# First gate projection by pairs of row chunks (0 and 2, then 1 and 3) through a strided moving operand, with the late transposes copied by two engines

## Chip, cores, metric

One core of one Trainium2 chip. The metric is the device time of one execution in microseconds (us); the span of a trace is about 1.3 us shorter. Before: 164.19 us, median of three runs (164.17 to 164.63). A change counts as faster or slower beyond 2%.

In the traces PE is TensorE, PEld its weight loads, DVE VectorE, ACT ScalarE, and SP the engine that issues most of the DMAs. Tile `pt` is a transposed chunk in PSUM, `xT` its copy in SBUF, `pw` the output of the warm-ups. k counts the five pieces of 128 input columns (KD = 5); the chunks of 128 rows are numbered 0 to 3.

## The reference

```python
def reference(x, w_gate, w_up, w_down):      # x 1x2048x640, w_gate and w_up 640x1536, w_down 1536x640, all bf16
    g = silu(x @ w_gate)
    u = x @ w_up
    return (g * u) @ w_down
```

## The kernel before

The kernel works on four blocks of 512 rows of x; in each, twelve times, a gate projection `pg` (5 matmuls, one for each 128 of the 640 input columns), an up projection `pu`, silu on ScalarE, a product on VectorE; then the down projection. The x of blocks 1 to 3 is transposed by DMA. The 512 rows of block 0 come as four chunks of 128 rows, are transposed on TensorE and copied out of PSUM, because the first matmul waits for them. Warm-up matmuls on a tile of ones fill TensorE until data are there. "Second block" below means the second 128 columns of the weights, that is the second pg and pu.

```python
    N_WARM = 20
    W_CHUNKS = [(0, 1), (1, 3), (3, 6), (6, 9), (9, 12)]
    # ... (tiles and views cut)
    queues = (nc.sync, nc.scalar)
    halves = ((0, KD // 2 + 1), (KD // 2 + 1, KD))
    for c in (0, 1):                                   # SP: chunks 0, 1; ACT: chunks 2, 3
        for i, eng in enumerate(queues):
            load_x(eng, c + 2 * i, c + 2 * i + 1)
    for dst, src in ((wg_sb, wg_v), (wu_sb, wu_v)):    # weights of the first block
        for eng, (k0, k1) in zip(queues, halves):
            eng.dma_start(out=dst[:, k0:k1, wslice(0, 1)], in_=src[:, k0:k1, wslice(0, 1)])
    load_w(nc.sync, wg_sb, wg_v, *W_CHUNKS[1])         # second and third block
    # ... (silu table, further loads, helpers cut)

    def transpose_chunk(c, parts):
        c_sl = slice(c * P, (c + 1) * P)
        for copy, tag, k0, k1 in parts:
            pt = psum.tile([P, k1 - k0, P], bf16, tag=tag, name="pt")
            for kd in range(k0, k1):
                nc.tensor.transpose(out=pt[:, kd - k0, :],
                                    in_=x_sb[:, c, kd * P : (kd + 1) * P], identity=ident[:])
            copy(out=xT[:, k0:k1, c_sl], in_=pt[:])

    # ... in the loop, first projection only:
                h = (SUB - 1) * P
                warm(N_WARM)
                for n, c in enumerate((0, 2, 1)):
                    transpose_chunk(c, [(nc.vector.tensor_copy, ("po_a", "po_b")[n % 2], 0, KD)])
                transpose_chunk(SUB - 1, [(nc.vector.tensor_copy, "po_b", 0, 2),
                                          (nc.scalar.copy, "po_a", 2, KD)])
                warm(2)
                proj(pg, wg_sb, fc, sb, 0, h)          # columns of chunks 0, 1, 2
                proj(pg, wg_sb, fc, sb, h, S_BLK)      # chunk 3
                proj(pu, wu_sb, fc, sb, 0, S_BLK)
```

## Time and profile before

| | before |
|---|---|
| time (median), span of the trace | 164.19 us, 163.1 us (of an execution of 164.41 us) |
| TensorE busy | 159.1 us (98%) |
| first gate matmul starts | 5.39 us |
| second block's first up matmul starts | 8.64 us |
| from there to the end | 154.46 us |

### The profile page before, as it was taken

The page shows a single profiled execution, that of the slowest core. Times are in us where ns is not written, and L with a number is a line of the kernel's source. Part 1 is how long each engine was busy: PE and PEld are TensorE (multiplying, and loading weights), DVE is VectorE, ACT ScalarE, POOL GpSimd, SP SyncE. Part 2 cuts the span into 40 slices and gives each one's busy share as a digit, 9 for nine tenths or more (in the row PEclk, how much of TensorE's full clock was granted, in tenths as well). Part 3 has the DMA queues.
Part 4 walks back from the last instruction along what each step waited for, and adds up shares of the span by engine and source line. Part 5 has one row for each costly group of instructions (what it writes and reads, how often), then busy time and mean ns, then how long its engine had stood idle before and what let it go on. Part 6 is the DMA issues. An engine that isn't in the chain of part 4 may idle for free.

```text
span 163.1 us, 1864 instructions
## 1 busy us (share of the span) xinstructions
PE 159.1 (98%) x764; PEld 75.2 (46%) x779; DVE 37.8 (23%) x58; ACT 42.2 (26%) x71; POOL 0.6 (0%) x6
## 2 busy tenths in 40 slices
PE   8899999999999999999999999999999999999994
PEld 7544444444444444444444444444444444445442
DVE  2323333310013333311003333331001333332000
ACT  3222222212232222221222222221214222222121
POOL 1000000000000000000000000000000000000000
DMA  7999999803200000003110000000320000000312
GB/s 212 274 333 330 361 245 187 152 6 60 67 32 0 0 0 0 4 0 34 64 64 0 2 4 0 0 0 3 62 68 32 0 0 0 0 0 4 54 34 72
DMA packets 26888, 11.26 MB, mean 69 GB/s; under 512 B 17664, under 2 KB 26880, under 8 KB 26880
## 3 DMA queue, kind: packets, MB, share of 16 engines
q1 hardware_dynamic: 17968, 10.16, 22.9%
q10 hardware_dynamic: 8912, 0.98, 3.9%
q8 instruction: 6, 0.10, 0.3%
q14 instruction: 2, 0.02, 0.0%
HBM read 6.55 MB, written 2.62 MB: 56 GB/s over the span
## 4 chain that ended last, share of the span: by engine, by line
PE 95%; DMA 2%; issue 1%; DVE 0%; SPq 0%
PE pg L134 32%; PE pu L134 31%; PE po_a L204 25%; PE po_t L180 6%; DMA x_sb<-in_x_dram 2%; PE po_b L217 0%; PE pt L125 0%; DVE xT L130 0%; SPq L74 0%; DVE ot_b L225 0%
## 5 line engine op out<-in xcount | busy, mean ns | idle before, releaser
L134 PE MATMUL pg<-xT,wg_sb 128*128 128x512 bf16 (+2 forms) x245 | 59.7, 375 | 0.2 <-DVE xT L130 0.2
L134 PE MATMUL pu<-xT,wu_sb 128*128 128x512 bf16 x230 | 59.0, 379 | 0.5
L172 DVE TENSOR_TENSOR aT<-sg,pu 128x512 bf16<-128x512 f32 x48 | 33.0, 687 | 100.8 <-PE pu L134 100.8
L171 ACT ACTIVATE sg<-pg 128x512 f32<-128x512 f32 x48 | 28.7, 597 | 71.1 <-PE pg L134 71.1
L204 PE MATMUL po_a<-wd_sb,aT 128*128 128x512 bf16 x188 | 41.9, 379 | 0.2
L134 PEld LDWEIGHTS <-wg_sb 128*128 128x128 bf16 x245 | 23.8, 98 | 28.4 <-DMA wg_sb<-in_w_gate_dram 0.4
L134 PEld LDWEIGHTS <-wu_sb 128*128 128x128 bf16 x240 | 23.4, 98 | 28.1
L204 PEld LDWEIGHTS <-aT 128*128 128x128 bf16 x192 | 18.8, 98 | 22.5
L212 ACT CAST ot<-po_a 128x512 bf16<-128x512 f32 x16 | 9.4, 585 | 32.4 <-PE po_a L204 19.2
L180 PE MATMUL po_t<-aT,wd_sb 128*128 128x512 bf16 (+1 forms) x47 | 10.3, 366 | 0.1
L180 PEld LDWEIGHTS <-wd_sb 128*128 128x128 bf16 x48 | 4.7, 98 | 5.1
L189 ACT CAST ot_t<-po_t 128x512 bf16<-128x512 f32 (+1 forms) x4 | 2.2, 558 | 11.6 <-PE po_t L180 11.6
L190 DVE STREAM_TRANSPOSE ot_q<-ot_t 128x512 bf16<-128x512 bf16 (+1 forms) x4 | 2.7, 678 | 9.1 <-ACT ot_t L189 9.1
L103 PE MATMUL pw<-ones 128*128 128x128 bf16 x22 | 2.6, 302 | 0.4 <-DVE ones L78 0.4
L225 DVE CAST ot_b<-po_b 128x128 bf16<-128x128 f32 x1 | 0.3, 292 | 9.9 <-PE po_b L217 9.9
L125 PE MATMUL pt<-ident,x_sb 128*128 128x128 bf16 x20 | 2.0, 269 | 0.5 <-DMA x_sb<-in_x_dram 0.5
L130 DVE COPY xT<-pt 128x640 bf16<-128x640 bf16 (+1 forms) x4 | 1.7, 439 | 3.5 <-PE pt L125 3.5
L103 PEld LDWEIGHTS <-ones 128*128 128x128 bf16 x22 | 2.2, 139 | 0.4 <-DVE ones L78 0.4
L125 PEld LDWEIGHTS <-x_sb 128*128 128x128 bf16 x20 | 1.6, 122 | 0.9 <-DMA x_sb<-in_x_dram 0.8
L89 ACT ACT_TABLE_LOAD x1 | 1.3, 1283 | 2.0 <-issue 2.0
L130 ACT COPY xT<-pt 128x384 bf16<-128x384 bf16 x1 | 0.5, 479 | 1.6 <-PE pt L125 1.6
L217 PEld LDWEIGHTS <-aT 128*128 128x128 bf16 x12 | 0.8, 98 | 0.2
(9 smaller groups left out, 2.1 us busy)
## 6 DMA issues: line engine op xcount, KB each, us to landing
out_dram<-ot SPq DMA_DIRECT2D x16, 128.0 KB, 1.7
wd_sb<-in_w_down_dram SPq DMA_DIRECT2D x1, 1920.0 KB, 11.8
wg_sb<-in_w_gate_dram SPq DMA_DIRECT2D x3, 480.0 KB, 7.1
wu_sb<-in_w_up_dram SPq DMA_DIRECT2D x3, 480.0 KB, 7.8
out_dram<-ot_q ACTq DMA_DIRECT2D x12, 32.0 KB, 1.9
x_sb<-in_x_dram SPq DMA_DIRECT2D x2, 160.0 KB, 3.1
x_sb<-in_x_dram ACTq DMA_DIRECT2D x2, 160.0 KB, 3.3
wg_sb<-in_w_gate_dram SPq DMA_DIRECT2D x1, 320.0 KB, 4.3
```

The source lines that it names most:

```text
L89: nc.scalar.activation(silu_first[:], ones[:, 0:1], ACT.Silu)
L103: nc.tensor.matmul(pw[:, 0:P], lhsT=ones[:], rhs=ones[:], start=True, stop=True)
L125: nc.tensor.transpose(out=pt[:, kd - k0, :], in_=x_sb[:, c, kd * P : (kd + 1) * P], identity=ident[:],)
L130: copy(out=xT[:, k0:k1, c_sl], in_=pt[:])
L134: nc.tensor.matmul(ps[:, c0:c1], lhsT=w_sb[:, kd, fc * P : (fc + 1) * P], rhs=xT[:, kd, sb * S_BLK + c0 : sb * S_BLK + c1], start=(kd == 0 ...
L171: nc.scalar.activation(sg[:], pg[:], ACT.Silu)
L172: nc.vector.tensor_tensor(out=aT[:, fc, s_sl], in0=sg[:], in1=pu[:], op=ALU.mult)
L180: nc.tensor.matmul(po_t[:], lhsT=wd_sb[:, kf, DA:D], rhs=aT[:, kf, sb * S_BLK : sb * S_BLK + n_t], start=(kf == 0), stop=(kf == KF - 1),)
L189: nc.scalar.copy(ot_t[:], po_t[:])
L190: nc.vector.transpose(out=ot_q[:], in_=ot_t[:])
L204: nc.tensor.matmul(po_a[:], lhsT=aT[:, kf, s0 : s0 + P], rhs=wd_sb[:, kf, 0:DA], start=(kf == 0), stop=(kf == KF - 1),)
L212: nc.scalar.copy(ot[:], po_a[:])
```

## The change

Its intent: start the gate projection on the two chunks that arrive first (0 and 2), while the copies of the two late ones (1 and 3) still run, and let ScalarE and VectorE share these copies. Four warm-ups move into the gap before the late chunks. The assertion on SUB is left out here.

```diff
-    N_WARM = 20
+    N_WARM, N_GAP = 18, 4
...
+    def proj_pair(ps, w_sb, fc, sb, b):
+        def pair(ap):
+            return ap.rearrange("p (a b c) -> p b a c", b=2, c=P)[:, b]
+        for kd in range(KD):
+            nc.tensor.matmul(
+                pair(ps[:]),
+                lhsT=w_sb[:, kd, fc * P : (fc + 1) * P],
+                rhs=pair(xT[:, kd, sb * S_BLK : (sb + 1) * S_BLK]),
+                start=(kd == 0),
+                stop=(kd == KD - 1),
+            )
...
-                h = (SUB - 1) * P
+                dve, act = nc.vector.tensor_copy, nc.scalar.copy
                 warm(N_WARM)
-                for n, c in enumerate((0, 2, 1)):
-                    transpose_chunk(
-                        c, [(nc.vector.tensor_copy, ("po_a", "po_b")[n % 2], 0, KD)]
-                    )
-                transpose_chunk(
-                    SUB - 1,
-                    [
-                        (nc.vector.tensor_copy, "po_b", 0, 2),
-                        (nc.scalar.copy, "po_a", 2, KD),
-                    ],
-                )
+                transpose_chunk(0, [(dve, "po_a", 0, KD)])
+                transpose_chunk(2, [(dve, "po_b", 0, KD)])
+                warm(N_GAP)
+                for c in (1, 3):
+                    transpose_chunk(c, [(act, "po_a", 0, 2), (dve, "po_b", 2, KD)])
                 warm(2)
-                proj(pg, wg_sb, fc, sb, 0, h)
-                proj(pg, wg_sb, fc, sb, h, S_BLK)
+                proj_pair(pg, wg_sb, fc, sb, 0)
+                proj_pair(pg, wg_sb, fc, sb, 1)
                 proj(pu, wu_sb, fc, sb, 0, S_BLK)
```

## The prediction

> **What bounds the kernel now.** I read the page's busy table and chain first, then the waits of the two TensorE rows, then the first 8 us in order of time, because the diff touches only what runs before the second projection.
>
> From the page:
>
> ```profile
> PE 159.1 (98%) x764; PEld 75.2 (46%) x779; DVE 37.8 (23%) x58; ACT 42.2 (26%) x71; POOL 0.6 (0%) x6
> ...
> PE 95%; DMA 2%; issue 1%; DVE 0%; SPq 0%
> ```
>
> TensorE is busy for 98% of the 163.1 us span and carries 95% of the chain that ended last. The waits of PE over the whole run are 0.4 us at the start, 0.5 us for x, and this, its only wait after 5.3 us:
>
> ```profile
> PE pg L134 <- DVE xT L130: 0.2, 1, 0.2
> ```
>
> So past 5.39 us TensorE is a solid row: a change in the start can only move that row rigidly, by the change in the moment when the first up projection (pu) starts. The chain at the start:
>
> ```profile
> 0.46 3.81 DMA x_sb<-in_x_dram
> 4.26 0.05 issue
> 4.31 0.51 PE pt L125 x5
> 4.82 0.02 issue
> 4.84 0.50 DVE xT L130
> 5.35 0.04 issue
> 5.39 1.25 PE pg L134 x10
> ```
>
> Read alone, this says: x chunk 1 lands at 4.27, five transposes, a 0.50 us VectorE copy, then the gate projection. That is what the change attacks. But the row of weight loads over 4.2 to 7.7 us says something the chain hides:
>
> ```profile
> 4.30 0.60 PEld L125 LDWEIGHTS <-x_sb 128*128 128x128 bf16 x10 [0.80 <-DMA x_sb<-in_x_dram]
> 4.87 0.15 PEld L103 LDWEIGHTS <-ones 128*128 128x128 bf16 x2
> 5.37 1.09 PEld L134 LDWEIGHTS <-wg_sb 128*128 128x128 bf16 x10 [0.35 <-DMA wg_sb<-in_w_gate_dram]
> ```
>
> The first gate weights were themselves awaited: the load started at 5.37, released by the DMA of w_gate, 0.02 us before the matmul that the copy released. Two waits end together, and the chain shows only the later. The landings confirm it (issue start plus time to landing, from the views of the issues): w_gate k 0 to 2, issued 0.91, 4.4 us, lands 5.31; k 3 and 4, issued 1.03, 4.5 us, lands 5.53. The w_up pieces: issued 1.39, 4.9 us, lands 6.29; issued 1.52, 4.5 us, lands 6.02. The x chunks: 0 at 2.5, 2 at 2.83, 1 at 4.27, 3 at about 4.5. (Times to landing are rounded to 0.1 us.)
>
> Could the weights come sooner? The 16 DMA engines are full meanwhile (columns: PE, PEld, DVE, ACT, POOL busy, clock, DMA share, GB/s):
>
> ```profile
> 2.50:3.60 1.10, 1.10 (x12) 1.01 (x10) 0.32 (x1) 1.03 (x2) 0.00 (x0) 1.00 1.04 313
> 3.60:4.30 0.70, 0.18 (x2) 0.00 (x0) 0.66 (x2) 0.00 (x0) 0.00 (x0) 1.00 1.03 233
> ```
>
> and the diff touches no transfer.
>
> **What the Trainium skill says.** "TensorE: Matmul & The Clock Gate", section "Back-to-back issue gap": an isolated warm gap of N/2.4 + 2.5 ns. The trace agrees with that form: 5 matmuls of 512 columns take 1.08 us in the chain, 216 ns each; and pg's 5x384 + 5x128 from 5.39 to the last result at 6.64 fit 5x162.5 + 5x55.8 = 1.09 us of gaps plus the drain. I use 109 ns for N=256 (an estimate by that formula). The same page, Part 1: the clock is at half rate until about 3.4 us of sustained activity, in a free-running window. The trace agrees: the 20 warm-up matmuls from 0.40 run (2.31-0.30)/19 = 106 ns apart, the ten transposes from 4.31 about 60 ns apart, although the clock column reads 1.00 for all of them; so the release came between 3.5 and 4.3 us. "SBUF — State Buffer", section "Door 1: The DMA port swizzle": non-contiguous PSUM access slows matmuls because PSUM lines are 8 bytes, SBUF lines 16. Here the runs are 128 elements, 512 bytes in PSUM and 256 in SBUF, with one jump each, so I expect no cost; no run of before shows it.[...]
>
> **The change, part by part.**
>
> 1. Warm-ups 20 to 18. They end at about 0.40 + 18x0.107 = 2.33 instead of 2.54. Chunk 0 lands at 2.5, so its transposes still start at about 2.5. Worth 0.0, leaving an idle gap of up to 0.2 us.
> 2. Chunks 0 and 2: as before, two VectorE copies of 492 ns, ending about 3.8 and 4.3.
> 3. Four gap warm-ups at 107 ns: from about 3.6 to 4.0, inside the 0.53 us in which PE waited for chunk 1 (4.31). Cost 0, as long as they end before 4.3.
> 4. Chunks 1 and 3: same 10 transposes, 4.31 to 4.87 in starts. Copies: ScalarE takes 256 elements of each chunk, VectorE 384. From ScalarE's 479 ns for 384 and 597 for its 512-wide silu, (597-479)/128 = 0.92 ns per element, so 256 cost about 361 (estimate; other shape and function). VectorE: 281 for 256, 492 for 640, 0.55 ns per element, so 384 cost about 351. ScalarE: chunk 1 from 4.65 to 5.01, chunk 3 from 5.03 to 5.39. VectorE: 4.84 to 5.19, then 5.20 to 5.55. Before, the last copy ended at 5.12 + 0.48 = 5.60. So the copies finish 0.05 earlier: small in itself.
> 5. The projection by pairs: ten of N=256 in place of five of 384 and five of 128. Streaming 10x109 = 1.09 us against 1.09: equal. Pair 0 needs chunks 0 and 2 only (copied by 4.3), so xT is out of its way. Were the copies all, pair 0 would start when PE is through the transposes and 2 warm-ups, about 4.98 instead of 5.39: the intended gain is 0.41 us.
> 6. But pair 0 needs w_gate, at 5.31 plus the about 0.04 between a landing and its use (x chunk 1: 4.27 to 4.31). It starts at 5.36 to 5.37. Its k 3 would come at 5.37 + 3x0.109 = 5.70, after 5.53: no second wait. Pair 1 starts at 5.92, later than its copies (5.55): no wait. The pair ends at 5.37 + 1.09 = 6.46, where pu starts (before: 5.39 + 1.09 = 6.48; 7.56 for the next pg minus 1.08 confirms it, a pu record is missing). w_up lands at 6.29: no wait.
>
> Sum: 0.00 + 0.00 + 0.00 + 0.02 = 0.02 us of gain. All of the intended 0.41 but 0.02 goes into a wait for w_gate that was always behind the copy. If nothing but the dependency tracking spoiled the stride (pair 0 treated as columns 0 to 384, thus waiting for chunk 1's copies until 5.19), the result is the same, since 5.19 is before 5.37.
>
> **Rivals.**
>
> A. The weights land sooner without the profiler or in another run. For it: landings of DMA vary, and the copies end right where w_gate lands, so on some runs the copy alone binds. Against: DMA share above 1 in the stretches before. Its ceiling: pair 0 at 4.98, pair 1 at 5.53 (its copies at 5.39 and 5.55 just in time), pu at 6.07, but w_up holds pu to about 6.33, so 0.15 us; with all weights early 0.41 us. Time 163.8 to 164.05. I give it one in four.
>
> B. The stride costs. If a jump in PSUM and SBUF halved the rate, 10x109 would become 2.18 us: +1.09, 165.3. Against it: only one jump in 256 columns, so the runs are dozens of lines of either memory long. One in thirty.
>
> C. The clock is released later: 18 warm-ups leave a gap at 2.33 to 2.5 and the free-running window may then not count as busy. If the half rate lasted one more window of 3.4 us from 4.3, it would cost up to about half of the busy work there: some 1.2 to 1.7 us, 165.4 to 165.9. Against: a gap below 0.2 us where before there was one of 0.53 at 3.78, which the four gap warm-ups now shorten. One in twenty.
>
> D. ScalarE's two copies delay its first silu: no, it starts at 6.68 in before, more than 1 us after them, and TensorE does not wait for it.
>
> **Range and chances.** Centre: 164.19 - 0.02, with a quarter of rival A's 0.15 to 0.4 (about -0.05): 164.12. The three runs of before lie between 164.17 and 164.63, so noise of 0.2 to 0.4 us exceeds the effect. Range 163.80 to 164.50, that is from nearly all of the intended gain to a run like before's slowest. Faster by over 2% means under 160.9 us, 3.3 us away: the stretch up to pu's start is 6.48 us in all, and eight times the intended gain is needed; 0.5%. Slower by 2% means above 167.5: B and C together would make about 2.6 us; 0.5%.
>
> **What would show it right or wrong.** Right: PE's first pg matmul in the changed kernel starts at 5.35 to 5.40 and its idle time is ended by the DMA of wg_sb, not by a copy; that idle time is longer than 0.19 (about 0.4 us, from 5.0); ten pg matmuls of 128x256, then pu 1.09 us after the first of them; ScalarE shows two 128x256 copies near 0.36 us, and neither pair waits for any. Step 3 is right if PE's wait for x before the chunk 1 transposes shrinks from 0.53 to about 0.1. Wrong, towards faster: pg starts before 5.2, so w_gate landed sooner than I read it. Wrong, towards slower: starts more than 0.12 us apart in the ten pair matmuls (B or C; C if the transposes from 4.3 are still 107 ns apart), or a new wait of PE after 6.5 us. The whole is wrong if the time leaves the range with the start of pu unmoved: then something after it changed.

## The result, and the profile after

164.04 us (163.77 to 164.19, six runs) against 164.28 us (164.16 to 164.63, six runs): ratio 0.9981, 95% interval 0.9967 to 0.9995. Ratios here are the mean time of one kernel's fast runs over that of the other's of the same rounds, so not quite the ratio of the medians that stand beside them. By the 2% rule: the same. Taken alone the interval says "0.3 us faster"; the experiments ask whether that stands.

The chain of the changed kernel over its first 10 us (start, length, what; a matmul piece counts from the result before it, so pg's issue began at 5.05):

```profile
0.46 3.87 DMA x_sb<-in_x_dram
4.33 0.05 issue
4.37 0.73 PE pt L125 x10
5.10 0.11 PE pw L103 x2
5.21 1.09 PE pg L149 x10
```

The VectorE copy has left the chain: transposes, warm-ups and gate projection follow each other without a wait. The weight loads and copies of the same stretch, in order of time (idle time before and what ended it in brackets):

```profile
4.69 0.65 ACT L130 COPY xT<-pt 128x256 bf16<-128x256 bf16 x2 [1.16 <-PE pt L125]
4.86 0.64 DVE L130 COPY xT<-pt 128x384 bf16<-128x384 bf16 x2 [0.67 <-PE pt L125]
5.00 1.03 PEld L149 LDWEIGHTS <-wg_sb 128*128 128x128 bf16 x10
7.25 0.76 PEld L134 LDWEIGHTS <-wg_sb 128*128 128x128 bf16 x5 [0.35 <-DMA wg_sb<-in_w_gate_dram]
```

The wait for the first gate weights, [0.35 <-DMA wg_sb] in the trace of before, is missing at 5.00. A new one stands at 7.25: the second block's gate weights. (These are idle times of the row of weight loads, which partly overlap the matmuls before; at 7.25 the matmuls themselves stood still for 0.03 us.) The first half of the answer is in the list of DMA issues (KB, us to landing), first of the kernel before, then of the changed one:

```profile
wg_sb<-in_w_gate_dram SPq DMA_DIRECT2D x1, 96.0 KB, 4.4
```

```profile
wg_sb<-in_w_gate_dram SPq DMA_DIRECT2D x1, 96.0 KB, 3.9
```

Issued at 0.91 in both, the first gate weights landed at 5.31 in one trace and at 4.81 in the other, and no line of the diff touches them. The groups by shape show the rest as foretold:

```profile
L149 PE MATMUL pg<-xT,wg_sb 128*128 128x256 bf16 x10 | 1.3, 272 | 0.0
L130 ACT COPY xT<-pt 128x256 bf16<-128x256 bf16 x2 | 0.7, 372 | 1.2 <-PE pt L125 1.2
L130 DVE COPY xT<-pt 128x384 bf16<-128x384 bf16 x2 | 0.6, 358 | 0.7 <-PE pt L125 0.7
```

The starts of the ten pair matmuls lie 109 to 110 ns apart. The first up matmul began at 6.14 (its record is missing; 6.035 + 0.109) instead of 6.48, the second block's at 8.34 instead of 8.64, and the span fell by 0.28 us. The second block's up matmuls, before and changed:

```profile
8.64 1.24 PE L134 MATMUL pu<-xT,wu_sb 128*128 128x512 bf16 x5
8.34 1.24 PE L134 MATMUL pu<-xT,wu_sb 128*128 128x512 bf16 x5
```

So in this pair of traces the time went where the change aimed. The question is whether it is the change or the two executions.

### The profile page after: what moved, and what is told of

It reads as the page before. It is cut to its first block, busy times and chain, and to the rows that moved or that the text cites. A ratio compares the mean times of both kernels' runs of the same rounds, so it can differ in the third digit from the quotient of the medians.

```text
span 162.8 us, 1869 instructions
## 1 busy us (share of the span) xinstructions
PE 159.0 (98%) x766; PEld 75.3 (46%) x781; DVE 37.9 (23%) x58; ACT 42.4 (26%) x72; POOL 0.6 (0%) x6
## 4 chain that ended last, share of the span: by engine, by line
PE 96%; DMA 2%; issue 1%; SPq 0%; DVE 0%
PE pu L134 31%; PE pg L134 31%; PE po_a L213 25%; PE po_t L189 6%; DMA x_sb<-in_x_dram 2%; PE pg L149 1%; PE pt L125 0%; PE po_b L226 0%; SPq L74 0%; DVE ot_b L234 0%; PE pw L103 0%
## 5 line engine op out<-in xcount | busy, mean ns | idle before, releaser
L134 PE MATMUL pg<-xT,wg_sb 128*128 128x512 bf16 x235 | 58.4, 379 | 0.0
L213 PEld LDWEIGHTS <-aT 128*128 128x128 bf16 x192 | 18.8, 98 | 22.6
L149 PE MATMUL pg<-xT,wg_sb 128*128 128x256 bf16 x10 | 1.3, 272 | 0.0
```

What stands on the lines that cost most here:

```text
L134: nc.tensor.matmul(ps[:, c0:c1], lhsT=w_sb[:, kd, fc * P : (fc + 1) * P], rhs=xT[:, kd, sb * S_BLK + c0 : sb * S_BLK + c1], start=(kd == 0 ...
L149: nc.tensor.matmul(pair(ps[:]), lhsT=w_sb[:, kd, fc * P : (fc + 1) * P], rhs=pair(xT[:, kd, sb * S_BLK : (sb + 1) * S_BLK]), start=(kd == ...
L213: nc.tensor.matmul(po_a[:], lhsT=aT[:, kf, s0 : s0 + P], rhs=wd_sb[:, kf, 0:DA], start=(kf == 0), stop=(kf == KF - 1),)
```

## The experiments

Twelve runs, on another chip. Theory: the start is decided by things that differ from execution to execution and are not in the diff (when x and the weights land, when TensorE's clock is released), and the change wins only where x lands late and the weights early. Rival: a real gain of 0.3 us.

### before_again and after_again: both kernels unchanged

No edit.

> The kernel before, unchanged, for a second trace. Theory 1 (the landing of the first gate weights scatters from execution to execution, whatever the kernel; the 5.31 us of the first trace was a late one): w_gate k 0 to 2 lands between 4.7 and 5.4 us, most likely near 4.9, and then the first weight load isn't what PE waits for; the first gate matmul still starts at 5.35 to 5.45, held by VectorE's copy of chunk 1. Theory 2 (the change itself made the weights land sooner, by 0.5 us): w_gate lands at 5.25 to 5.40 again.

> The changed kernel, unchanged. Ratio 0.998 (0.997 to 0.9995), that is 0.2 to 0.45 us less than before. Theory 1: w_gate k 0 to 2 lands somewhere in 4.7 to 5.4 us, not always at 4.81; first gate matmul at 5.05 if it lands before 5.0, else 0.03 to 0.05 after the landing. Theory 2: 4.75 to 4.90 again.

before_again: 164.12 us. after_again: 164.23 us (163.85 to 164.72), ratio 0.9999 (0.9979 to 1.0018), outside the 0.997 to 0.9995 that I expected. Both traces differ from the first two in x: chunk 1 landed at 3.36 and 3.46 instead of 4.27 and 4.33. before_again, weight loads in order of time:

```profile
4.85 1.11 PEld L134 LDWEIGHTS <-wg_sb 128*128 128x128 bf16 x10 [0.34 <-DMA wg_sb<-in_w_gate_dram]
5.91 0.80 PEld L134 LDWEIGHTS <-wu_sb 128*128 128x128 bf16 x5
7.24 0.76 PEld L134 LDWEIGHTS <-wg_sb 128*128 128x128 bf16 x5 [0.52 <-DMA wg_sb<-in_w_gate_dram]
```

The kernel before started its gate projection at 4.88 here, 0.17 earlier than the changed one in its first trace, and then waited at 7.24 for the second block's weights, just as the changed one had at 7.25. Without the change it got the same span, 162.8 us. Theory 2 (the change brings the weights) falls: w_gate landed at 4.81 without it. My expectation that the copy of chunk 1 would hold the matmul until 5.35 was wrong as well, since I had taken the late x for given. The chain of after_again:

```profile
2.63 1.25 PE pt L125 x10
3.88 0.43 PE pw L103 x4
4.31 0.67 PE pt L125 x10
4.98 0.11 PE pw L103 x2
5.09 1.16 PE pg L149 x10
```

With chunk 1 there at 3.46, the four gap warm-ups (0.43 us at the slow clock) are now a link of the chain: they hold back transposes whose data had come.

### copies_only and pairs_only: each part alone

copies_only, on the changed kernel:

```diff
-                proj_pair(pg, wg_sb, fc, sb, 0)
-                proj_pair(pg, wg_sb, fc, sb, 1)
+                proj(pg, wg_sb, fc, sb, 0, 3 * P)
+                proj(pg, wg_sb, fc, sb, 3 * P, S_BLK)
```

> Warm-ups, transposes and copies of the change, projection of before (384 columns, then 128). The first piece then needs chunk 1's copies, which ended at 5.06 and 5.22 in the changed kernel, so the first gate matmul starts at about 5.26 against 5.39 and 5.05: if the early landing of the weights is usual (theory 1), a gain of 0.13 us (ratio 0.9992) and a wait of about 0.2 us ended by VectorE's copy; if the split copies are what matters (rival), the whole 0.3 us (0.998).

pairs_only, on the changed kernel:

```diff
-    N_WARM, N_GAP = 18, 4
+    N_WARM = 20
...
-                warm(N_GAP)
-                for c in (1, 3):
-                    transpose_chunk(c, [(act, "po_a", 0, 2), (dve, "po_b", 2, KD)])
+                transpose_chunk(1, [(dve, "po_a", 0, KD)])
+                transpose_chunk(3, [(dve, "po_b", 0, 2), (act, "po_a", 2, KD)])
```

> Projection by pairs alone; 20 warm-ups, no gap warm-ups and the copies of before. Pair 0 starts at 5.05 as in the changed kernel. Pair 1 reaches k 0 at 5.60, when chunk 1's copy (5.35) and VectorE's part of chunk 3 (about 5.55 plus 0.04) are just in, and k 2 at 5.82, after ScalarE's 5.60: no wait or one below 0.05 us. So theory (the pairs are all of the gain): as after_again within 0.1 us, ratio 0.998. Rival (the split copies are needed for it): a wait of PE of 0.1 us or more before pair 1 and a gain of at most 0.2 us (0.9988).

copies_only: 164.66 us (164.32 to 165.30), 1.0025 (1.0005 to 1.0045): slower, where both theory and rival foretold a gain. pairs_only: 164.15 us (163.93 to 164.61), 0.9989 (0.9975 to 1.0004). Both expectations were built on the late x of the first traces, and neither can be read off: in both traces something else takes over. (The traced execution of pairs_only, 164.61 us, is the slowest of its six; the others took 163.93 to 164.18.) TensorE over the first 9 us of pairs_only:

```profile
2.50 2.34 PE L125 MATMUL pt<-ident,x_sb 128*128 128x128 bf16 x20
4.63 0.42 PE L103 MATMUL pw<-ones 128*128 128x128 bf16 x2
4.94 1.90 PE L149 MATMUL pg<-xT,wg_sb 128*128 128x256 bf16 x10
```

The ten pair matmuls took 1.90 us instead of 1.25. Their starts lie 213 ns apart until 6.19 and 109 ns from 6.35: TensorE's clock was at half rate until about 6.3 us. In the first trace of the changed kernel it had been released at about 3.5. Pair 0 did start at 4.94, early as expected; the cold clock then took back more than that. copies_only was cold until about 5.9. The means are 164.77 for copies_only and 164.19 for pairs_only, 0.58 us apart and more than a kernel strayed from itself (0.14%, 0.23 us, see before_copy); but with one trace each, both cold, these runs don't show why, nor which of the two parts is worth what.

### after_third and no_gap: the gap warm-ups

no_gap, on the changed kernel:

```diff
-                warm(N_GAP)
```

> The changed kernel once more, since the first comparison gave 0.9981 and the second 0.9999. Theory A (the gain depends on when x chunk 1 lands: 4.3 us in the first two traces, 3.24 to 3.46 in the four of the other chip; where it lands early, the gate weights of 4.8 to 5.0 us hold both kernels): ratio 0.998 if its trace shows chunk 1 landing after 4.2, 0.999 to 1.001 if before 3.7. Rival B (the gain is real everywhere and the second comparison was unlucky): 0.998 either way.

> The changed kernel without the four gap warm-ups. Theory A: if chunk 1 lands before 3.7, those four (0.22 us warm, 0.43 cold) stood on TensorE's own path, but the gate weights at 4.8 to 5.0 us then hold the first gate matmul: 0.0 to 0.2 us less than after_third; if it lands after 4.2, no difference at all within 0.1 us. Rival C (the gap warm-ups keep the clock released): the clock is released a window later in more executions, 0.2 to 0.6 us more than after_third, and a wider scatter.

after_third: five runs of 163.95 to 164.54, 1.0012 (0.9994 to 1.0029); the sixth, the profiled one, of 439 us, is left out (see the end). Its DMA records can still be read: chunk 1 landed at 3.26, for which theory A expected 0.999 to 1.001; 1.0012 just misses that, and its interval excludes rival B's 0.998. no_gap: 164.02 us (163.93 to 164.18), 0.9995 (0.9980 to 1.0009). The means are 164.33 and 164.05, so no_gap is 0.28 us lower (0.0 to 0.2 was expected) and scatters less; but the intervals overlap, so a gain is not shown. Rival C, that the gap warm-ups keep the clock released, is not borne out: no_gap has no wider scatter and no higher mean, and its one trace is released at 3.8 us. Weight loads of no_gap:

```profile
4.76 0.99 PEld L149 LDWEIGHTS <-wg_sb 128*128 128x128 bf16 x10 [0.25 <-DMA wg_sb<-in_w_gate_dram]
7.13 0.76 PEld L134 LDWEIGHTS <-wg_sb 128*128 128x128 bf16 x5 [0.51 <-DMA wg_sb<-in_w_gate_dram]
```

Here is the predicted wait: with x early, pair 0 stands still for w_gate (landing 4.71), though the matmuls themselves for 0.08 us only. And the second block's weights again cap what the first block won.

### gate_late: the wait for w_gate made certain

On the changed kernel:

```diff
-    for dst, src in ((wg_sb, wg_v), (wu_sb, wu_v)):
+    for dst, src in ((wu_sb, wu_v), (wg_sb, wg_v)):
         for eng, (k0, k1) in zip(queues, halves):
```

> The changed kernel with the first w_up pieces issued ahead of the first w_gate pieces, so that w_gate lands when w_up did (5.3 to 6.3 us). If the wait foretold (pair 0 held by the landing of w_gate) is real when the weights are late: first gate matmul 0.03 to 0.05 after w_gate k 0 to 2 lands, at 5.35 to 5.9, its idle time ended by the DMA of wg_sb, and 0.2 to 0.6 us more than after_third (ratio to before 1.000 to 1.003). If the weights never matter: as after_third within 0.1 us.

164.52 us (164.29 to 164.71), 1.0021 (1.0005 to 1.0037). The mean is 0.19 us above after_third's, just short of the 0.2 to 0.6 expected and within the scatter (the intervals overlap). The trace has the wait in the place and with the releaser named:

```profile
5.37 1.28 PEld L149 LDWEIGHTS <-wg_sb 128*128 128x128 bf16 x10 [0.25 <-DMA wg_sb<-in_w_gate_dram]
```

w_gate landed at 1.39 + 3.9 = 5.29, the first gate matmul began at 5.38. So pair 0 is held by w_gate when that is late: the mechanism of the prediction is real. The wait is small: the last warm-up began at 5.09 and, at the cold spacing of 107 ns, the first gate matmul could have begun at 5.19, so 0.19 us are lost to w_gate. TensorE was cold here until about 6.0 and came late by itself.

### early_w and small_chunks: the second block's weights

early_w, on the changed kernel:

```diff
-        for eng, (k0, k1) in zip(queues, halves):
-            eng.dma_start(out=dst[:, k0:k1, wslice(0, 1)], in_=src[:, k0:k1, wslice(0, 1)])
+        load_w(nc.sync if dst is wg_sb else nc.scalar, dst, src, *W_CHUNKS[0])
```

> The changed kernel with the first w_gate slice as one DMA from SP and the first w_up slice as one from ACT: two DMAs fewer ahead of the next weights, so the ninth DMA, which was issued only at 2.8 to 3.0 us, 0.4 after x chunk 0 landed, is now a later one and the weights of the second block are issued at about 1.9 and land earlier than 7.2 us. Theory D (in early-release executions the second block's w_gate at 7.2 us takes back part of the gain, as PE's waits of 0.41 us in before_again and 0.03 in the first trace of the changed kernel show): no wait before the second gate projection, 0.1 to 0.3 us less than after_third. Rival: the earlier big transfers share the DMA engines with the first slices and delay these by as much: same or slower.

164.83 us (164.06 to 165.09), 1.0037 (1.0016 to 1.0058): slower, so theory D brought nothing in this form. (The 0.41 us that the expectations of early_w and small_chunks give for before_again is the extra idle time of the weight loads; the matmuls waited 0.19 us, as in the table below.) In its trace the second block's w_gate landed at 6.95 and nothing waits for it, but the first w_gate landed at about 5.0 and the first gate matmul waited 0.21 us for it. That trace is of the fastest of its six runs, so why the other five took 0.6 to 1.0 us more is open.

small_chunks, on the changed kernel:

```diff
-    W_CHUNKS = [(0, 1), (1, 3), (3, 6), (6, 9), (9, 12)]
+    W_CHUNKS = [(0, 1), (1, 2), (2, 3), (3, 6), (6, 9), (9, 12)]
```

> The changed kernel with the weights of the second and third blocks loaded one block at a time instead of two together. Theory D (in executions with an early clock release, the second block's gate weights, landing at 7.1 to 7.2 us, take back what the first block won): its w_gate lands 0.3 to 0.6 us sooner, PE's idle time before the second gate projection (0.41 us in before_again, 0.19 in no_gap) is gone, and the time is 0.05 to 0.3 us below after_fourth. Rival (the start is bound by bytes that have to come in any case, and rows of 256 bytes cost as much as they save; or a later block waits instead): within 0.1 us of after_fourth, or slower.

164.28 us (163.73 to 164.81), 0.9996 (0.9972 to 1.0020); the mean is 0.22 us below after_fourth's, which is within the scatter. Its second gate weights landed at about 6.4 instead of 7.47, and its second block followed the first with no wait, where after_fourth waited 0.20 us for them. But the second gate projection starts at the same time in both traces, small_chunks first:

```profile
7.51 1.24 PE L134 MATMUL pg<-xT,wg_sb 128*128 128x512 bf16 x5
7.51 1.25 PE L134 MATMUL pg<-xT,wg_sb 128*128 128x512 bf16 x5
```

small_chunks' TensorE was cold until about 5.45 and came to its second block only at 7.51, so weights at 7.47 would hardly have held it either. The earlier landing is shown; that it removes a wait, or gains time, is not, and no version here clearly beats the kernel before.

### before_copy and after_fourth: the null comparison

No edit.

> The kernel before against itself: a null comparison, to see how far such a ratio strays. If the gap of 0.9981 to 1.0012 between three comparisons of one and the same pair of kernels is the scatter of the executions, this ratio lies within 0.998 to 1.002 too, with runs between 163.8 and 164.7 us. If the comparisons are good to 0.0005 and the changed kernel really differs from chip to chip, it lies within 0.9995 to 1.0005.

> The changed kernel a fourth time. Theory (no gain on average, the clock's release and the landings decide each execution): ratio 0.999 to 1.001, the mean of the four within 0.0007 of 1. Rival (a real gain of 0.3 us as first measured): 0.998. In its trace the first up matmul starts at 5.97 to 6.7, and the second block's up at 8.2 to 8.9; span minus the latter is 154.4 to 154.5 as in all traces before.

before_copy, the kernel before against itself: 0.9986 (0.9969 to 1.0003), medians 164.11 and 164.27. after_fourth: 164.56 us (164.15 to 164.72), 1.0011 (0.9991 to 1.0031), a little above the 0.999 to 1.001 expected. A comparison of a kernel with itself strays by 0.0014, so one of 0.9981 is weak evidence by itself. The four of the changed kernel, 0.9981, 0.9999, 1.0012 and 1.0011, average 1.0001. The rival in its plain form, a gain of 0.3 us everywhere, falls: two of the four intervals exclude 0.998 (0.9994 to 1.0029 and 0.9991 to 1.0031). A gain that comes only where x chunk 1 lands late (4.27 and 4.33 in the first two traces) is neither shown nor excluded: no later trace of either kernel had a landing after 4.0, so this half of the theory rests on the first pair alone.

before_copy's chain names the gate weights, in a kernel without the change:

```profile
0.91 4.13 DMA wg_sb<-in_w_gate_dram
5.04 0.05 issue
5.09 1.26 PE pg L134 x10
```

### no_warm_at_all: how much the clock's release is worth

On the changed kernel:

```diff
-    N_WARM, N_GAP = 18, 4
+    N_WARM, N_GAP = 0, 0
```

> The changed kernel without the 18 and the 4 warm-ups. Theory (the clock is released[...]; so far it came between 3.4 and 6.3 us): PE is busy only from 2.45, so the release comes between 5.3 and 9 us, and each us of cold work after the first gate matmul costs about half a us: 0.4 to 1.5 us more than before (ratio 1.003 to 1.009), with a scatter of over 0.7 us between runs. Rival (the release follows a fixed time of activity and what scatters is only the DMA): a constant loss, scatter as before, below 0.5 us.

165.28 us (164.44 to 165.46), 1.0048 (1.0025 to 1.0071), a spread of 1.0 us. Loss (0.79 us in the means) and spread are in the ranges expected from the release theory, and the rival's loss below 0.5 us is not what was seen. The spread tells little: eleven runs of the kernel before spread by 0.81 us. The trace:

```profile
5.13 1.93 PE L149 MATMUL pg<-xT,wg_sb 128*128 128x256 bf16 x10
6.90 1.24 PE L134 MATMUL pu<-xT,wu_sb 128*128 128x512 bf16 x5
```

TensorE was cold until about 6.5 in pg, inside the 5.3 to 9 us expected and nearly as in pairs_only.

### All traces together

Landings are issue start plus time to landing (given to 0.1 us, so good to about 0.05); "released" is where the spacing of the matmuls halves; all in us.

| trace | x chunk 1 lands | w_gate (k 0 to 2) lands | clock released | first pg matmul | wait before second pg | second pu starts | span |
|---|---|---|---|---|---|---|---|
| before | 4.27 | 5.31 | 4.4 | 5.39 | 0 | 8.64 | 163.1 |
| before_again | 3.36 | 4.81 | 4.15 | 4.88 | 0.19 | 8.33 | 162.8 |
| before_copy | 3.3 | 5.04 | 4.15 | 5.09 | 0.21 | 8.57 | 163.0 |
| changed | 4.33 | 4.81 | 3.5 | 5.05 | 0.03 | 8.34 | 162.8 |
| after_again | 3.46 | 4.9 | 4.4 | 4.98 | 0 | 8.24 | 162.7 |
| after_fourth | 3.46 | 4.8 | 4.9 | 5.14 | 0.20 | 8.60 | 163.1 |
| pairs_only | 3.24 | 4.9 | 6.3 | 4.94 | 0 | 8.84 | 163.3 |
| copies_only | 3.26 | 4.9 | 5.9 | 5.19 | 0 | 8.78 | 163.2 |

In all thirteen fast traces, the five others included, span minus the start of the second pu is 154.44 to 154.48 us. So the differences between executions, and between these kernels, are made before 9 us. In the last column but one the kernel before ranges from 8.33 to 8.64 and the changed kernel from 8.24 to 8.60: two executions of one kernel differ by as much as the two kernels do.

## Why the prediction was right or wrong

- **Where the effect can lie** (only in the moment pu starts): right, and sharper than I put it, by the constant 154.46 us.
- **Step 1, 18 warm-ups**: right. Chunk 0's transposes began at 2.46 against 2.51, after a gap of 0.17 us.
- **Step 3, gap warm-ups cost nothing**: right in the first trace (issued 3.50 to 3.66, chunk 1 landing at 4.33), wrong as a general statement: with chunk 1 at 3.46, after_again's chain contains them with 0.43 us. And the foretold shrinking of the wait for x from 0.53 to 0.1 did not come: the wait was 0.49. The clock was released at 3.5 and the four took 56 ns apiece, not 107, which makes 0.2 us; chunk 1 also landed 0.06 later, the transposes had begun 0.05 earlier, and at the faster clock the last matmul before the wait ended sooner after its start.
- **Step 4, copies**: right, 372 and 358 ns against 361 and 351.
- **Step 5, ten of 256 columns stream as fast as five of 384 and five of 128**: right, starts 109 to 110 ns apart. Rival B falls. The intended gain was summed a little too high: in the trace of before the last warm-up starts at 4.98, so pair 0 could follow at 5.03, and the gain is 0.36 us, not 0.41.
- **Step 6, pair 0 is held by w_gate at 5.36**: this step failed in the trace of the result. w_gate landed at 4.81, not 5.31, and pg began at 5.05, right behind the warm-ups: rival A's case. pu started 0.34 us earlier where the sum said 0.02; rival A's cap of 0.15 us by w_up did not bind, as both w_up pieces had landed by 5.5. The mechanism itself is shown by gate_late and no_gap and, without the change, by before_copy; what was off is that I took one landing for a property of the program. It ranged from 4.61 to 5.31 in the fast traces that left the first eight loads as they were.
- **"No wait before the second block"**, implied by adding the gain through to the end: wrong. That wait is 0.03 us in the result and about 0.2 in four other traces; where pg starts early it gives back a part.
- **Rival C**, a later clock release: I had it as a risk of this change, one in twenty. It came at 4.15 to 4.4 in three traces of the kernel before, at 3.5 to 4.9 in three of the changed one, and as late as 6.3 in variants that kept warm-ups. (For the trace of before the prediction says between 3.5 and 4.3, from an average spacing; the single spacings put it at about 4.4.) That the gap at 2.33 triggers a late release was not shown: the latest one was in pairs_only, whose TensorE program up to the first gate matmul is that of the kernel before. Whether the change shifts the release on average stays open.
- **Time and range**: 164.12 foretold, 164.04 measured, all six runs but one within 163.80 to 164.50. The mean gain over four comparisons is 0.0 us, near the 0.02 of the sum. That the sum fits is in part luck, since it comes out for a mixture of reasons: in some executions w_gate holds both kernels, in others the clock or the second block's weights do, and in the first the intended 0.3 us appeared.

What stays open: whether the change gains where x lands late, the worth of each part by itself, the slowness of early_w and copies_only in most of their runs, and why x chunk 1 landed near 4.3 us in the first two traces and before 4.0 in the others.

## What to carry to other kernels

A start that waits for a copy, a weight load and a clock within 0.1 us of each other has no single bound: moving one of them uncovers the next, and the next differs from run to run, so read landings and matmul spacing in several traces of the same kernel before crediting a change of the first microseconds. When an effect is below 0.3%, compare the kernel with itself as well; here that null comparison strayed by 0.14%, and the interval of the first comparison, 0.9967 to 0.9995, lies wholly below the mean of all four, 1.0001. A filler placed "in a gap" is free only while the gap is there: when its data come earlier, it is on the path.

## What the Trainium skill lacked or had wrong

- "TensorE: Matmul & The Clock Gate", Part 1, says that the window of 3.4 us is free-running and that the release varies by about 0.5 us between runs. Here it varied by 1.4 us among three traces of the changed kernel (3.5 to 4.9) and by 2.8 us among all that kept warm-ups (3.5 to 6.3 us). The page does not say which busy share makes a window count. An estimate from its window length: pairs_only's window up to about 2.9 us, with TensorE busy from 0.40 (73%), did not count; before's up to 4.4, with a gap of 0.74 us (78%), did.
  It knows clock shares of 4/8, 8/8, 13/16 and, once, a quarter for 50 us. The profiled execution of after_third ran slow from end to end, 437.8 us, with three matmuls of 128 columns in 432 ns, 144 ns each against 56, 0.39 of the full rate: an estimated 3/8. Its group of gate matmuls:

```profile
L134 PE MATMUL pg<-xT,wg_sb 128*128 128x512 bf16 x235 | 151.4, 835 | 0.0
```

- "SBUF — State Buffer", "Door 1: The DMA port swizzle": any non-contiguous PSUM pattern is said to slow matmuls significantly. Two runs of 512 bytes with one jump cost nothing: 109 to 110 ns per 256 columns, between 56 for 128 and 162 to 163 for 384.
- "TensorE: Matmul & The Clock Gate", Part 1, warns in general that recorded clock events can be unreliable; no page that I read says that the granted clock in a profile can read 1.00 throughout while matmuls of 128 columns start 107 ns apart and later 56. It read 1.00 in every trace here, in the slow one too.
